# Loading small inputs as two rows each, and spreading them over the partitions with TensorE, in a one-token attention and mixer kernel

## The chip, the cores and the metric

The kernel runs on one core of a Trainium2 chip. The metric is device time in microseconds (us); lower is better.

## The reference, cut to what matters

```python
A: x (1,1,1024), k_cache and v_cache (1,4,65536,128), wq (1024,4096), wo (4096,1024)   # attention
B: B_x (1,1,1024), w_in (1024,3584), w_sp (1,1), b_sp (1,), w_out (1792,1024)          # gated MLP
gate_w (1024,)                                                                          # all bf16

x = A_x
g = sigmoid((x * gate_w).sum(-1))
a = softmax(x @ wq @ k.T / sqrt(128)) @ v @ wo         # 32 query heads, 4 KV heads
z = gelu(x @ w_in);  z1, z2 = halves of z
b = (z1 * (w_sp * layernorm(z2) + b_sp)) @ w_out
out = g * a + (1 - g) * b
```

There is one token. Nearly all the work is to read 162 MB of caches and weights once. The small inputs are x and gate_w (2 KB each) and the scalars w_sp and b_sp (2 bytes each).

## The kernel before

The big arrays go through a ring of five SBUF slots of up to 4 MB. SP issues their loads on its own DMA queue (q1), a load as soon as its slot has been used. ACT issues the four small loads at the start on another queue (q10). Every access is to one tensor called arena, so the profile tells inputs apart by the DRAM side or by line number.

```python
NS = 5                                    # slots in the ring
...
def small(dst, src, key): ...             # one DMA on ACT's queue
# x and gate_w: partition p gets elements 4p..4p+3 of each half: 256 pieces of 8 bytes
small(vw(xT, 0, [[4, 2], [1, 4]]), A_x[0, 0].rearrange("(i p k) -> p i k", i=2, k=4), "xT")
small(vw(gw, 0, [[4, 2], [1, 4]]), gate_w.rearrange("(i p k) -> p i k", i=2, k=4), "gw")
# the scalars: one element of DRAM read 128 times, once for each partition
small(wb[:, 0:1], bass.AP(tensor=B_w_sp.tensor, ..., ap=[[0, 128], [1, 1]]), "wsp")
small(wb[:, 1:2], bass.AP(tensor=B_b_sp.tensor, ..., ap=[[0, 128], [1, 1]]), "bsp")
...
# the first work, in program order (each engine works in this order)
DVE: z2 = xT * gw                         # L384, waits for x and gate_w
DVE: gs = sum over the free axis
PE:  sum over the partitions (matmul with ones)
ACT, DVE: g = 1 / (1 + exp(-gs)), 1 - g
DVE: xw = spread xT                       # L395
PE:  64 matmuls x @ wq                    # L404; they free the first two slots of the ring
...
DVE: transposes of the K tiles            # L449
PE:  scores                               # L457
```

Order of the loads: wq, wq, K, w_in, K, w_in, K, w_out, K, ..., then K and V in turn, then wo in six pieces.

## Time and profile before

| | before |
|---|---|
| time, median of 6 runs beside the changed kernel | 387.72 us (387.49 to 388.95) |
| span of the profiled execution | 385.9 us |
| small packets (q10) | 832 |
| x / gate_w / w_sp / b_sp landed, us after issue | 22.0 / 38.9 / 48.7 / 56.9 |
| wq matmuls start | 42.13 us |
| sixth load of the ring issued | 45.76 us |

From the page of the kernel before: its span; the DMA row (busy tenths in 40 slices of 9.65 us) and what the DMA engines moved in each slice; the queues, with packets, MB and share of 16 engines' time; and the chain of work that ended last, by engine.

```profile
span 385.9 us, 3595 instructions
...
DMA  8999999999999999999999999999999999999994
GB/s 326 435 435 442 374 442 426 429 436 433 435 408 419 435 435 430 428 435 427 431 431 435 433 435 431 435 423 429 435 431 426 428 432 435 430 431 428 419 419 190
...
q1 hardware_dynamic: 6200, 162.01, 98.1%
...
q10 hardware_dynamic: 832, 0.00, 0.1%
...
DMA 53%; PE 22%; DVE 22%; issue 1%; ACT 0%; ACTq 0%; DVEq 0%
```

The bulk queue occupies the DMA engines for 98.1% of the span. The stream is what the time consists of. Low slices are the fifth (38.6 to 48.2 us: 374) and the twelfth and thirteenth (106 to 125 us: 408 and 419).

The DMA issues of the four small loads: destination and source, issuing queue, size, and us from issue to landing.

```profile
arena<-in_A_x_dram ACTq DMA_DIRECT2D x1, 2.0 KB, 22.0
arena<-in_gate_w_dram ACTq DMA_DIRECT2D x1, 2.0 KB, 38.9
arena<-in_B_w_sp_dram ACTq DMA_DIRECT2D x1, 0.2 KB, 48.7
arena<-in_B_b_sp_dram ACTq DMA_DIRECT2D x1, 0.2 KB, 56.9
```

The chain of waits in order of time (start, duration, what), some of its pieces:

```profile
1.24 38.87 DMA arena<-in_gate_w_dram
...
42.13 6.39 PE pb L404 x64
...
51.27 1.26 DVE arena L449
...
371.10 11.62 DMA arena<-in_A_wo_dram
...
382.76 0.62 PE pb L635 x7
383.41 0.42 DVE arena L641
```

The chain begins with 39 us of waiting for 2 KB of gate_w, and ends with the last piece of wo. SP's own timeline shows how the ring bridges the first part: five loads at the start, the next only once the wq matmuls have freed a slot.

```profile
2.77 0.49 SPq L345 DMA_DIRECT2D arena<-in_A_k_cache_dram  x1
45.76 0.33 SPq L345 DMA_DIRECT2D arena<-in_B_w_in_dram  x1
48.54 0.33 SPq L345 DMA_DIRECT2D arena<-in_A_k_cache_dram  x1
```

### The profile page before, as it was taken

The page shows a single profiled execution, that of the slowest core. Times are in us where ns is not written, and L with a number is a line of the kernel's source. Part 1 is how long each engine was busy: PE and PEld are TensorE (multiplying, and loading weights), DVE is VectorE, ACT ScalarE, POOL GpSimd, SP SyncE. Part 2 cuts the span into 40 slices and gives each one's busy share as a digit, 9 for nine tenths or more (in the row PEclk, how much of TensorE's full clock was granted, in tenths as well). Part 3 has the DMA queues.
Part 4 walks back from the last instruction along what each step waited for, and adds up shares of the span by engine and source line. Part 5 has one row for each costly group of instructions (what it writes and reads, how often), then busy time and mean ns, then how long its engine had stood idle before and what let it go on. Part 6 is the DMA issues. An engine that isn't in the chain of part 4 may idle for free.

```text
span 385.9 us, 3595 instructions
## 1 busy us (share of the span) xinstructions
PE 227.0 (59%) x1542; PEld 84.7 (22%) x1542; DVE 210.5 (55%) x326; ACT 30.6 (8%) x71; POOL 2.1 (1%) x9
## 2 busy tenths in 40 slices
PE   0000668983886888472688383827883929543354
PEld 0000225562232222121222120212220202211121
DVE  4000078335999997574597574735984748511010
ACT  1000000001011110000010000000010100320000
POOL 2000000000000000000000000000000000000000
PEclk9999969695899999696789697956697978866555
DMA  8999999999999999999999999999999999999994
GB/s 326 435 435 442 374 442 426 429 436 433 435 408 419 435 435 430 428 435 427 431 431 435 433 435 431 435 423 429 435 431 426 428 432 435 430 431 428 419 419 190
DMA packets 7048, 162.24 MB, mean 420 GB/s; under 512 B 1524, under 2 KB 1528, under 8 KB 1784
## 3 DMA queue, kind: packets, MB, share of 16 engines
q1 hardware_dynamic: 6200, 162.01, 98.1%
q8 instruction: 12, 0.20, 0.2%
q10 hardware_dynamic: 832, 0.00, 0.1%
q14 instruction: 4, 0.03, 0.0%
HBM read 162.01 MB, written 0.00 MB: 420 GB/s over the span
## 4 chain that ended last, share of the span: by engine, by line
DMA 53%; PE 22%; DVE 22%; issue 1%; ACT 0%; ACTq 0%; DVEq 0%
DMA arena<-in_A_k_cache_dram 31%; DVE arena L449 16%; PE pb L457 13%; DMA arena<-in_gate_w_dram 10%; DMA arena<-in_A_v_cache_dram 9%; PE pb L543 3%; DMA arena<-in_A_wo_dram 3%; PE pb L501 2%; DVE arena L470 2%; PE pb L404 2%; DVE arena L492 1%; PE pb L635 1%; DVE arena L518 0%; DVE arena L438 0%; PE pb L523 0%
## 5 line engine op out<-in xcount | busy, mean ns | idle before, releaser
L457 PE MATMUL pb<-arena 128*128 128x512 bf16 x512 | 154.4, 442 | 78.5 <-DVE arena L449 76.2
L449 DVE STREAM_TRANSPOSE arena<-arena 128x1024 f32<-128x1024 f32 x128 | 151.3, 1216 | 56.7 <-DMA arena<-in_A_k_cache_dram 50.5
L457 PEld LDWEIGHTS pb<-arena 128*128 128x128 bf16 x512 | 45.4, 106 | 181.9 <-DVE arena L449 128.1
L501 PE MATMUL pb<-arena 128*32 128x512 bf16 x512 | 39.3, 442 | 20.3 <-DMA arena<-in_A_v_cache_dram 17.8
L487 ACT ACTIVATE arena<-arena 128x512 bf16<-128x512 f32 x32 | 23.0, 720 | 208.5 <-DVE arena L492 155.3
L492 DVE STREAM_TRANSPOSE arena<-arena 128x512 bf16<-128x512 bf16 x32 | 21.7, 679 | 18.3 <-PE pb L501 18.3
L470 DVE TENSOR_SCALAR_CACHE_REDUCE arena<-pb 128x512 f32<-128x512 f32 x32 | 21.7, 678 | 5.7 <-PE pb L457 5.5
L386 PE MATMUL pb<-arena 128*128 128x1 f32 x2 | 0.6, 364 | 40.6 <-DVE arena L385 40.6
L501 PEld LDWEIGHTS pb<-arena 128*32 128x32 bf16 x512 | 12.9, 107 | 44.5 <-issue 36.5
L384 DVE TENSOR_TENSOR arena<-arena 128x8 f32<-128x8 bf16 x1 | 0.2, 166 | 35.1 <-DMA arena<-in_gate_w_dram 35.1
L543 PEld LDWEIGHTS pb<-arena 128*128 128x128 bf16 x224 | 13.8, 161 | 0.4
L543 PE MATMUL pb<-arena 128*128 128x1 bf16 x224 | 13.7, 198 | 0.0
L635 PE MATMUL pb<-arena 128*1 128x256 bf16 x128 | 7.8, 409 | 6.3 <-DMA arena<-in_A_wo_dram 6.2
L515 DVE RECIPROCAL arena<-pb 128x1 f32<-128x1 f32 x4 | 0.7, 168 | 18.1 <-PE pb L513 18.1
L386 PEld LDWEIGHTS pb<-arena 128*128 128x128 f32 x2 | 0.5, 314 | 40.6 <-DVE arena L385 40.6
L641 DVE TENSOR_TENSOR arena<-pb,arena 97x256 bf16<-97x256 f32 x1 | 0.4, 425 | 13.4 <-PE pb L635 13.4
L404 PE MATMUL pb<-arena 128*2 128x512 bf16 x64 | 6.4, 584 | 0.9 <-DVE arena L395 0.9
L487 ACT ACTIVATION_READ_ACCUMULATOR arena<-arena 128x1 f32 x32 | 6.0, 186 | 0.0
L635 PEld LDWEIGHTS pb<-arena 128*1 128x1 bf16 x128 | 3.4, 109 | 10.5 <-DMA arena<-in_A_wo_dram 7.6
L523 PE MATMUL pb<-arena 128*128 128x128 bf16 x16 | 1.8, 243 | 5.2 <-DVE arena L518 5.2
L554 DVE COPY arena<-pb 128x28 f32<-128x28 f32 x1 | 0.2, 187 | 7.8 <-PE pb L543 7.8
L411 DVE CAST arena<-pb 98x512 bf16<-98x512 f32 x1 | 0.7, 692 | 6.5 <-PE pb L404 6.5
(81 smaller groups left out, 47.7 us busy)
## 6 DMA issues: line engine op xcount, KB each, us to landing
arena<-in_A_k_cache_dram SPq DMA_DIRECT2D x16, 4096.0 KB, 28.8
arena<-in_A_v_cache_dram SPq DMA_DIRECT2D x16, 4096.0 KB, 33.5
arena<-in_A_wq_dram SPq DMA_DIRECT2D x2, 4096.0 KB, 17.0
arena<-in_B_w_in_dram SPq DMA_DIRECT2D x2, 3584.0 KB, 27.4
arena<-in_A_wo_dram SPq DMA_DIRECT2D x3, 2048.0 KB, 34.6
arena<-in_B_w_out_dram SPq DMA_DIRECT2D x1, 3584.0 KB, 16.8
arena<-in_A_wo_dram SPq DMA_DIRECT2D x1, 1024.0 KB, 23.1
arena<-in_A_wo_dram SPq DMA_DIRECT2D x2, 512.0 KB, 13.1
```

Source lines behind the costliest of these rows:

```text
L386: P("PE", lambda e: e.matmul(pf(PTB)[:, 0:1], ones, col(C_GS), start=True, stop=True), r=["ones", "gs"], w=[B(PTB)])
L404: ins = e.matmul(pf(OB)[32 * cg:32 * cg + 2, :], xw[:, 3 * c + 1 - s:3 * c + 3 - s], sl[:, WQ_N * k + 512 * (4 * s + cg):WQ_N * k + 512 * ...
L411: P("DVE", lambda e: e.tensor_copy(qsb[0:98, :], pf(OB)[0:98, :]), w=[("psb", 0), B(OB)])
L449: P("DVE", lambda e: e.transpose(ktb(i).bitcast(F32), sl[:, 2048 * j:2048 * (j + 1)].bitcast(F32)), r=[key], w=[("kt", i % NKTS)])
L457: ins = e.matmul(pf(sb), qpad[g % 2][:, o:o + 128], vw(ktb(i), 64 * f2 + ev, [[128, 16], [2, 32]]), start=(j == 0 and fe == 0), stop=(j == ...
L470: P("DVE", lambda e: e.tensor_scalar(scs(n), pf(sb), 0.0, None, op0=ALU.add, op1=ALU.max, accum_out=maxc[:, n:n + 1]), w=[("sc", n % NSC), ...
L487: P("ACT", lambda e: e.activation(psb(n), scs(n), ACTF.Exp, bias=gcol(g, K_NB), scale=SCALE, accum_out=lp[:, n:n + 1]), r=[("sc", n % NSC) ...
L492: P("DVE", lambda e: e.transpose(ptsb(n), psb(n)), r=[("psb", n % 2)], w=[("ptsb", n % 2)])
L501: ins = e.matmul(pf(OB)[32 * cg:32 * (cg + 1), :], ptsb(n)[:, 32 * b:32 * (b + 1)], vw(sl, 128 * b, [[2048, 4], [1, 128]]), start=(u == 0 ...
L523: ins = e.matmul(pf(MB)[:, 0:128], sel[:, 128 * c:128 * (c + 1)], osc[:, 128 * c:128 * (c + 1)], start=(c == 0), stop=(c == 3))
L543: ins = e.matmul(pf(MB)[:, z:z + 1], vw(sl, c0, [[FC, 128]]), xT[:, 2 * i + k:2 * i + k + 1], start=(i == 0 and k == 0 and z == 0), stop=( ...
L635: ins = e.matmul(pf(FB)[32 * q:32 * q + 1, 0:QW], ovec[:, 8 * i + c:8 * i + c + 1], sl[:, o:o + QW], start=(i == 0 and c == 0), stop=(i == ...
```

## The change

x and gate_w are loaded as two rows of 512 elements, on two partitions. Four PE transposes bring x to the partitions; the gate product and sum are done on the two rows. The scalars are loaded once each, and a matmul with a row of ones spreads them. The aim is to have the small inputs early and with few packets. The order at the start of the program becomes: transposes of x, spread of the scalars, gate product, gate sum, wq.

```diff
-    small(vw(xT, 0, [[4, 2], [1, 4]]), A_x[0, 0].rearrange("(i p k) -> p i k", i=2, k=4), "xT")
-    small(vw(gw, 0, [[4, 2], [1, 4]]), gate_w.rearrange("(i p k) -> p i k", i=2, k=4), "gw")
-    small(wb[:, 0:1], bass.AP(tensor=B_w_sp.tensor, offset=B_w_sp.offset, ap=[[0, 128], [1, 1]]), "wsp")
-    small(wb[:, 1:2], bass.AP(tensor=B_b_sp.tensor, offset=B_b_sp.offset, ap=[[0, 128], [1, 1]]), "bsp")
+    small(xrow[0:2, :], A_x[0, 0].rearrange("(i n) -> i n", i=2), KX)
+    small(grow[0:2, :], gate_w.rearrange("(i n) -> i n", i=2), KG)
+    small(wb[0:1, 0:1], B_w_sp, "wsp")
+    small(wb[0:1, 1:2], B_b_sp.rearrange("(a n) -> a n", a=1), "bsp")
...
-    P("DVE", lambda e: e.tensor_tensor(z2[:, 0:KC], xT, gw, ALU.mult), ...)
-    P("DVE", lambda e: e.tensor_reduce(col(C_GS), z2[:, 0:KC], AXX, ALU.add), ...)
-    P("PE", lambda e: e.matmul(pf(PTB)[:, 0:1], ones, col(C_GS), start=True, stop=True), ...)
+    for c in range(4):                                                  # PE
+        ins = e.transpose(pbf(PTB)[:, 2 * c:2 * c + 2], vw(xrow, c, [[4, 128]], 0, 2), idb[0:2, 0:2])
+    P("DVE", ... tensor_copy(xT <- PTB)) ;  P("DVE", ... tensor_copy(xw <- xT))
+    P("PE", lambda e: e.matmul(pf(MB)[:, 0:2], oneb[0:1, :], wb[0:1, :], start=True, stop=True),
+      r=["oneb", "wsp", "bsp"], w=[B(MB)])
+    P("DVE", lambda e: e.tensor_copy(wbb, pf(MB)[:, 0:2]), ...)
+    P("DVE", lambda e: e.tensor_tensor(prod[0:2, :], xrow[0:2, :], grow[0:2, :], ALU.mult), ...)
+    P("DVE", lambda e: e.tensor_reduce(col(C_GS)[0:2, :], prod[0:2, :], AXX, ALU.add), ...)
+    P("PE", lambda e: e.matmul(pf(PTB)[:, 0:1], ones[0:2, :], col(C_GS)[0:2, :], start=True, stop=True), ...)
...
-    ... wb[:, 0:1] ... wb[:, 1:2]          # later, in the mixer
+    ... wbb[:, 0:1] ... wbb[:, 1:2]
```

More of the change, by code (lines that the diff above doesn't have):

```diff
@@ L189, in bass_gated_mix__gqa_block_cached__mixer_gmlp__decode_kernel @@
         ("QPAD", 2 * 4 * QP), ("IDB", 128), ("IDF", 256), ("BM", 256), ("ONES", 256), ("SEL", 16 * 32),
-        ("M16", 32), ("M8", 16), ("M32", 64), ("MQ", 32), ("OT", 256), ("XT", KC), ("GW", KC), ("WB", 2), ("MAXC", 2 * G * NU), ("LP", 2 * G * NU),
+        ("M16", 32), ("M8", 16), ("M32", 64), ("MQ", 32), ("OT", 256), ("XT", KC), ("WB", 2), ("WBB", 4), ("ONEB", 128), ("MAXC", 2 * G * NU), ("LP", 2 * G * NU),
         ("COLS", 2 * 64), ("DM", 32), ("QT", 32), ("QALL", 128), ("XW", 3 * KC), ("OSC", 512), ("OV", OC), ("Z", 2 * 28), ("Z2", 2 * 28),
@@ L211, in bass_gated_mix__gqa_block_cached__mixer_gmlp__decode_kernel @@
     m32, mq, ot = af("M32", 32), af("MQ", 16), af("OT", 128)
-    xT, gw, wb = ab("XT", KC), ab("GW", KC), ab("WB", 2)
+    xT, wb, wbb, oneb = ab("XT", KC), ab("WB", 2), af("WBB", 2), ab("ONEB", 128)
     qpad = [ab("QPAD", 4 * QP, 4 * QP * i) for i in range(2)]
@@ L256, in bass_gated_mix__gqa_block_cached__mixer_gmlp__decode_kernel @@
     P("DVE", lambda e: e.memset(ones, 1.0), w=["ones"])
+    P("DVE", lambda e: e.memset(oneb, 1.0), w=["oneb"])
     P("DVE", lambda e: e.memset(brow, 0.0), w=["brow"])
@@ L267, in f @@
                 return e.dma_start(dst, src)
-        P("ACT", f, w=[key], dma=key)
-    small(vw(xT, 0, [[4, 2], [1, 4]]), A_x[0, 0].rearrange("(i p k) -> p i k", i=2, k=4), "xT")
-    small(vw(gw, 0, [[4, 2], [1, 4]]), gate_w.rearrange("(i p k) -> p i k", i=2, k=4), "gw")
-    small(wb[:, 0:1], bass.AP(tensor=B_w_sp.tensor, offset=B_w_sp.offset, ap=[[0, 128], [1, 1]]), "wsp")
-    small(wb[:, 1:2], bass.AP(tensor=B_b_sp.tensor, offset=B_b_sp.offset, ap=[[0, 128], [1, 1]]), "bsp")
+        P("ACT", f, w=[key], dma="l%s" % (key if isinstance(key, str) else key[1]))
+    xrow, grow, prod = ab("SC", 512, (NSC - 2) * 1024), ab("SC", 512, (NSC - 3) * 1024), af("SC", 512, (NSC - 4) * 512)
+    KX, KG, KP = [("sc", NSC - i) for i in (2, 3, 4)]
+    small(xrow[0:2, :], A_x[0, 0].rearrange("(i n) -> i n", i=2), KX)
+    small(grow[0:2, :], gate_w.rearrange("(i n) -> i n", i=2), KG)
+    small(wb[0:1, 0:1], B_w_sp, "wsp")
+    small(wb[0:1, 1:2], B_b_sp.rearrange("(a n) -> a n", a=1), "bsp")
     stream = []
@@ L381, in bass_gated_mix__gqa_block_cached__mixer_gmlp__decode_kernel, with f @@
           r=["idb"], w=[KSE])
-    P("DVE", lambda e: e.tensor_tensor(z2[:, 0:KC], xT, gw, ALU.mult), r=["xT", "gw"], w=["z2"])
-    P("DVE", lambda e: e.tensor_reduce(col(C_GS), z2[:, 0:KC], AXX, ALU.add), r=["z2"], w=["gs"])
-    P("PE", lambda e: e.matmul(pf(PTB)[:, 0:1], ones, col(C_GS), start=True, stop=True),
+    def f(e):
+        for c in range(4):
+            ins = e.transpose(pbf(PTB)[:, 2 * c:2 * c + 2], vw(xrow, c, [[4, 128]], 0, 2), idb[0:2, 0:2])
+        return ins
+    P("PE", f, r=[KX, "idb"], w=[B(PTB)])
+    P("DVE", lambda e: e.tensor_copy(vw(xT, 0, [[4, 2], [1, 4]]), vw(pbf(PTB), 0, [[1, 2], [2, 4]])),
+      w=["xT", B(PTB)])
+    P("DVE", lambda e: e.tensor_copy(vw(xw, 1, [[3, KC]]), xT), r=["xT"], w=["xw"])
+    P("PE", lambda e: e.matmul(pf(MB)[:, 0:2], oneb[0:1, :], wb[0:1, :], start=True, stop=True),
+      r=["oneb", "wsp", "bsp"], w=[B(MB)])
+    P("DVE", lambda e: e.tensor_copy(wbb, pf(MB)[:, 0:2]), w=["wbb", B(MB)])
+    P("DVE", lambda e: e.tensor_tensor(prod[0:2, :], xrow[0:2, :], grow[0:2, :], ALU.mult), r=[KX, KG], w=[KP])
+    P("DVE", lambda e: e.tensor_reduce(col(C_GS)[0:2, :], prod[0:2, :], AXX, ALU.add), r=[KP], w=["gs"])
+    P("PE", lambda e: e.matmul(pf(PTB)[:, 0:1], ones[0:2, :], col(C_GS)[0:2, :], start=True, stop=True),
       r=["ones", "gs"], w=[B(PTB)])
@@ L392, in bass_gated_mix__gqa_block_cached__mixer_gmlp__decode_kernel @@
       r=["g"], w=["omg"])
-    P("DVE", lambda e: e.tensor_copy(vw(xw, 1, [[3, KC]]), xT), r=["xT"], w=["xw"])
     for i in range(4):
@@ L576, in mixer_piece @@
         P("DVE", lambda e: e.reciprocal(col(C_R1), col(C_S1)), r=["s1"], w=["r1"])
-        P("DVE", lambda e: e.scalar_tensor_tensor(col(C_AL), col(C_R1), 2.0, wb[:, 0:1], op0=ALU.mult, op1=ALU.mult),
-          r=["r1", "wsp"], w=["al"])
-        P("DVE", lambda e: e.tensor_copy(col(C_BE), wb[:, 1:2]), r=["bsp"], w=["be"])
+        P("DVE", lambda e: e.scalar_tensor_tensor(col(C_AL), col(C_R1), 2.0, wbb[:, 0:1], op0=ALU.mult, op1=ALU.mult),
+          r=["r1", "wbb"], w=["al"])
+        P("DVE", lambda e: e.tensor_copy(col(C_BE), wbb[:, 1:2]), r=["wbb"], w=["be"])
         P("DVE", lambda e: e.tensor_scalar(z2[:, 0:FC], ze[:, 0:FC], col(C_AL), col(C_BE), op0=ALU.mult, op1=ALU.add),
```

## The prediction

> **What bounds it now.** The DMA stream. The page's queue list has the bulk queue at 98.1% of 16 engines for 162.01 MB; the stretch view shows 431 GB/s from 118 to 360 us[...]. At 431 GB/s the bytes alone need 376 of the 385.9 us. PE is busy 59%, DVE 55%.
>
> **What the small loads cost.** x and gate_w go out as 256 pieces of 8 bytes each; with the two broadcast scalars the small queue has 832 packets. In the DMA issues x lands after 22.0 us, gate_w after 38.9, the scalars after 48.7 and 56.9. [...] x has 16 packets per engine, and 16 turns behind 32 KB bulk packets of about 1.22 us (packet records) make 19.5 of its 22.0 us. So in the chain of waits gate_w ends at 40.1 us, DVE idles 35.1 us before the gate product, and the wq matmuls start at 42.13, though the wq loads landed at about 12 and 21. K transposes start at 51.27; their load was there from about 31.
>
> **Why nearly all of it is hidden.** The ring holds five loads, about 46 us of stream. The sixth was issued at 45.76 us, just as the ring ran dry. Against 431 GB/s the stretches 40 to 45 (419), 45 to 50 (400), 50 to 104 (428), 104 to 108 (410) and 108 to 118 us (421; compute still catching up) are short by 0.14, 0.36, 0.38, 0.19 and 0.23 us: 1.3 us together. The chain gives gate_w 10% of the span, but removing that does not remove 39 us; the stream binds instead.
>
> **What changes.** Removed: about 830 small packets, a few tenths of a us of stream at most. Added: four small PE transposes, a tiny matmul, two PSUM copies, and a product and a sum over 2x512 in place of 128x8: 2 to 3 us in series (similar ones take 0.2 to 0.7), before the first wq load lands, so free. x and gate_w should land 3 to 5 us after issue (one or two turns of 1.22 us plus the 2.5 us that 22.0 leaves), the scalars within about 8.
>
> **What the profile after should show.** DVE's wait on small loads under 8 us (35.1). wq matmuls from 11 to 13 us. Sixth load issued at 15 to 18 us (45.76). First K transpose at 30 to 33 us. The dips at 45 to 50 and 104 to 118 us gone. From about 150 us on both traces agree but for a shift of about 1 us; the last wo load still ends the kernel, then about 3 us of PE, DVE and store.
>
> **Predicted time:** 387.75 - 1.3 = 386.4 us, range 385.6 to 387.4. Chances: faster by over 2% 0.01, within 2% 0.97, slower 0.02.
>
> **What would make it wrong.** Early work could be slower than the stream: K-only stages need about 10.5 us of DVE per pair against 9.7 us of stream, and PE at half clock needs more; if the ring fills there, dips move rather than vanish. The two-row loads may hold back the few DMA engines they use, or wait longer than one turn. If the deficit at 104 to 118 us is of the first V loads, not of the backlog, only about 0.9 us is gained.

From the prediction: 0.14 + 0.36 + 0.38 + 0.19 + 0.23 = 1.3 us, each from the stretch view. That the stream binds rests there on the 98.1% and the 376 us of bytes, and that small loads wait by turns on the packets of x. The half clock of its last paragraph is in the trace of before: from 85.2 to 98.9 us, for one, the granted clock was 0.5; a score matmul (L457) took 629 ns (median) at that clock and 378 at 1.0. Its few tenths of a us for the small packets are an estimate; the page has q10 at 0.1% of the 385.9 us, 0.4 us. Its 10.5 and 9.7 us are estimates too: eight transposes of 1.16 us and two reductions of 0.62 (from start to start at 59.50 to 64.77 us) make 10.5, and the 4.19 MB of a K load at 431 GB/s take 9.7.

## The result, and the profile after

| | before | after |
|---|---|---|
| median (range), 6 runs each | 387.72 us (387.49 to 388.95) | 386.63 us (386.58 to 386.90) |
| ratio, 95% interval | | 0.9969 (0.9956 to 0.9982) |
| small packets (q10) | 832 | 12 |
| wq matmuls start | 42.13 us | 15.25 us |
| sixth load issued | 45.76 us | 18.87 us |
| first K transpose | 51.27 us | 32.70 us |
| last piece of wo landed (chain of waits) | 382.72 us | 381.68 us |

A ratio is the mean time of one kernel's fast runs over that of the other's of the same rounds, so it is not quite the ratio of the medians quoted. The interval is a gain of 0.7 to 1.7 us, and the medians differ by 1.1 us.

The page of the changed kernel, the lines that answer to those of before:

```profile
span 384.9 us, 3607 instructions
...
GB/s 331 436 433 440 430 424 437 429 435 433 427 433 426 427 433 429 433 432 436 433 429 436 424 429 436 429 431 430 433 433 431 433 430 429 434 433 422 421 418 169
...
q1 hardware_dynamic: 6200, 162.01, 98.2%
...
q10 hardware_dynamic: 12, 0.00, 0.0%
...
DMA 71%; PE 16%; DVE 11%; issue 0%; SPq 0%
```

The fifth slice, 374 before, is 430; the twelfth and thirteenth, 408 and 419, are 433 and 426. The bulk queue's packets and bytes are the same.

The timeline of the start (start, duration, engine, line, operation, count, and the idle time before it with what ended it):

```profile
13.03 0.16 PE L396 MATMUL pb<-arena 1*128 1x2 bf16 x1 [10.14 <-DMA arena<-in_B_b_sp_dram]
13.23 0.16 DVE L398 COPY arena<-pb 128x2 f32<-128x2 f32 x1 [7.69 <-PE pb L396]
...
15.25 3.58 PE L419 MATMUL pb<-arena 128*2 128x512 bf16 x32
18.87 0.33 SPq L349 DMA_DIRECT2D arena<-in_B_w_in_dram  x1
23.00 3.21 PE L419 MATMUL pb<-arena 128*2 128x512 bf16 x32 [4.17 <-DMA arena<-in_A_wq_dram]
...
32.70 3.50 DVE L464 STREAM_TRANSPOSE arena<-arena 128x1024 f32<-128x1024 f32 x3 [3.71 <-DMA arena<-in_A_k_cache_dram]
```

All early work now waits for the bulk stream, except one thing: PE stands 10.14 us before the little matmul that spreads the scalars, for a b_sp that lands only at 13 us.

The end of the chain of waits:

```profile
370.06 11.62 DMA arena<-in_A_wo_dram
...
381.73 0.62 PE pb L650 x6
382.35 0.02 issue
382.37 0.42 DVE arena L656
```

It is the end of before, 1.04 us earlier. Nothing changed behind the last landing.

### Where in the stream the time was gained

The trace has records of the DMA packets; those of the bulk queue add up to the 162.01 MB that the page has as read. In the kernel before 4352 of its 6200 packets, with 88% of the bytes, are of 32 KB, and for 342 of the 385.9 us 16 bulk packets are under way at once, as one after another on each of 16 engines would give; a record does not name its engine. From these records, the time in us at which so many MB of the bulk queue had landed; 162.0 MB is the very end:

```
MB landed     before    after    gained
 10.0          26.91    26.54     0.38
 22.0          55.24    54.08     1.17
 44.0         106.63   105.56     1.07
 46.0         111.68   110.15     1.53
150.0         353.20   351.68     1.52
161.5         379.79   378.26     1.53
162.0         382.14   381.10     1.05
```

So the lead was gained before 112 us, and about a third of it did not survive to the last bytes. These are records of one execution each, and a single mark falls somewhere in a round of packets: b_swap (section 5), whose stream otherwise runs like that of before, is 0.3 us ahead at 46 MB and 0.05 at 47 MB. A difference of 0.2 to 0.3 us at one mark alone says nothing. Also from the records, the mean duration in ns of a bulk packet (scaled to 32 KB) by stretches of 4 us:

```
from us    4    8   12   16   20   24   28   32   36   40   44   48   52   56
before  1213 1228 1213 1213 1213 1213 1214 1217 1220 1247 1326 1231 1213 1213
after   1213 1213 1213 1213 1213 1213 1213 1213 1213 1221 1213 1216 1218 1239
```

Before has slow packets from about 42 to 49 us. It also has them at 104 to 112 us (1267 and 1259, where after has 1216), which is not in this table. The first place was the prediction's "ring running dry". But the records contradict that at once: in the kernel before, the fifth load was still landing until 51 us, and the sixth, issued at 45.76, was in time. Something else is slow there. What coincides with it is the w_sp load: its 128 small packets run from 40.3 us to about 50 us.

### The profile page after: what moved, and what is told of

It is laid out like the page before. It is cut to its first block, busy times and chain, and to the rows that moved or that the text cites. A ratio compares the mean times of both kernels' runs of the same rounds, so it can differ in the third digit from the quotient of the medians.

```text
span 384.9 us, 3607 instructions
## 1 busy us (share of the span) xinstructions
PE 233.6 (61%) x1547; PEld 86.2 (22%) x1547; DVE 211.6 (55%) x329; ACT 30.6 (8%) x71; POOL 2.1 (1%) x9
## 3 DMA queue, kind: packets, MB, share of 16 engines
q1 hardware_dynamic: 6200, 162.01, 98.2%
HBM read 162.01 MB, written 0.00 MB: 421 GB/s over the span
## 4 chain that ended last, share of the span: by engine, by line
DMA 71%; PE 16%; DVE 11%; issue 0%; SPq 0%
DMA arena<-in_A_k_cache_dram 59%; PE pb L472 11%; DMA arena<-in_A_v_cache_dram 10%; DVE arena L464 9%; DMA arena<-in_A_wo_dram 3%; PE pb L516 2%; PE pb L558 2%; DVE arena L485 1%; PE pb L650 1%; DVE arena L507 0%; DVE arena L533 0%; PE pb L538 0%; PE pb L528 0%; SPq L349 0%; PE pb L495 0%
## 5 line engine op out<-in xcount | busy, mean ns | idle before, releaser
L472 PE MATMUL pb<-arena 128*128 128x512 bf16 x512 | 160.0, 457 | 93.6 <-DVE arena L464 91.7
L472 PEld LDWEIGHTS pb<-arena 128*128 128x128 bf16 x512 | 46.7, 109 | 201.3 <-DVE arena L464 144.9
L558 PEld LDWEIGHTS pb<-arena 128*128 128x128 bf16 x224 | 13.8, 161 | 0.4
L656 DVE TENSOR_TENSOR arena<-pb,arena 97x256 bf16<-97x256 f32 x1 | 0.4, 425 | 13.4 <-PE pb L650 13.4
L650 PEld LDWEIGHTS pb<-arena 128*1 128x1 bf16 x128 | 3.4, 109 | 10.5 <-DMA arena<-in_A_wo_dram 7.6
```

The lines of the kernel that those rows point to most:

```text
L472: ins = e.matmul(pf(sb), qpad[g % 2][:, o:o + 128], vw(ktb(i), 64 * f2 + ev, [[128, 16], [2, 32]]), start=(j == 0 and fe == 0), stop=(j == ...
L558: ins = e.matmul(pf(MB)[:, z:z + 1], vw(sl, c0, [[FC, 128]]), xT[:, 2 * i + k:2 * i + k + 1], start=(i == 0 and k == 0 and z == 0), stop=( ...
L650: ins = e.matmul(pf(FB)[32 * q:32 * q + 1, 0:QW], ovec[:, 8 * i + c:8 * i + c + 1], sl[:, o:o + QW], start=(i == 0 and c == 0), stop=(i == ...
```

## The experiments

Two theories stood at first. "Cover" (the prediction's): the gain comes from work that starts earlier, so that the ring never runs short. "Packets": the gain comes from the small packets that are no longer sent, whatever the time at which work starts. The first four kernels ran on one chip beside the same nine runs of before (median 387.68 us).

### 1. Early start, all small packets kept (b_gate_late)

```diff
-    (gate product, sum, matmul, exp, ... before the wq matmuls)
+        if si == 1:          # after the scores of the second K tile
+            (the same gate product, sum, matmul, exp, ...)
```

> The kernel before, with all 832 small packets, but the gate chain (product, sum, matmul, exp) moved from before the wq matmuls to after the second K tile, so wq waits for x (about 22 us) and not for gate_w (about 40 us). Theory 'cover' (the gain comes from the bulk stream running short because work starts late): wq from about 22.5 us, sixth load at about 26 us, first K transpose at 31 to 33 us, no stretch under 425 GB/s between 40 and 120 us, time 386.8 to 387.1 us, so all of the gain but the 0.3 us of stream that the small packets take. Rival 'packets' (the gain comes from not sending the small packets, among them the shared w_sp element that is read 128 times from 40 to 51 us, just where the stream dips): the dip at 42 to 50 us stays at about 400 GB/s, time 387.4 to 387.7 us.

Measured: 387.85 us, ratio 1.0003 (0.9989 to 1.0017). No gain. SP's sixth load in the timeline of this run:

```profile
26.87 0.33 SPq L345 DMA_DIRECT2D arena<-in_B_w_in_dram  x1
```

The GB/s row of its page:

```profile
GB/s 326 435 435 430 387 435 430 428 436 435 433 431 435 435 419 431 428 435 427 428 431 431 433 428 435 435 433 436 428 431 426 428 432 424 433 435 435 414 420 168
```

The sixth load goes out 19 us earlier than before, and yet the fifth slice stays low (387). The bulk packets of 44 to 48 us took 1321 ns, before 1326. "Cover" falls as the explanation of that dip. The twelfth and thirteenth slices are full (431 and 435), and 0.5 us of lead is there from 46 MB on (111.18 us against 111.68), so the early start does something for that dip. But at the last byte the lead is gone: 382.16 against 382.14 us.

### 2. Late start, scalars loaded once (b_scal_new)

```diff
-    small(wb[:, 0:1], bass.AP(tensor=B_w_sp.tensor, ..., ap=[[0, 128], [1, 1]]), "wsp")
-    small(wb[:, 1:2], bass.AP(tensor=B_b_sp.tensor, ..., ap=[[0, 128], [1, 1]]), "bsp")
+    small(wb[0:1, 0:1], B_w_sp, "wsp")
+    small(wb[0:1, 1:2], B_b_sp.rearrange("(a n) -> a n", a=1), "bsp")
+    (spread by a matmul after q, read from wbb in the mixer, as in the change)
```

> The kernel before, with x and gate_w in 8-byte pieces as before, but the two scalars loaded once each and spread by a matmul (placed after q). Theory 'cover': wq still starts at about 42 us and the stream still dips at 42 to 50 and 104 to 118 us; time 387.4 to 387.7 us. Rival 'packets': the dip at 42 to 50 us is gone, since no w_sp reads fall there; time 386.9 to 387.2 us.

Measured: 387.08 us, ratio 0.9986 (0.9973 to 0.9998). SP's sixth load in the timeline:

```profile
45.94 0.33 SPq L347 DMA_DIRECT2D arena<-in_B_w_in_dram  x1
```

The GB/s row of the page:

```profile
GB/s 327 436 436 434 438 427 433 425 417 424 429 427 436 436 434 432 436 431 429 432 432 432 430 425 429 429 427 436 436 432 427 436 430 429 434 425 436 413 421 173
```

Work starts as late as before, and the fifth slice is full (438); the bulk packets of 44 to 48 us took 1216 ns. At 22 MB the stream is 0.76 us ahead of before. So the dip at 42 to 49 us belongs to the scalar loads. The dip at 104 to 118 us is gone too (427 and 436), and the lead grows there from 0.64 us at 44 MB to 1.08 at 46 MB, although work starts late. In the kernel before it was a near thing: the load issued at 105.14 us found, by an estimate from the sizes of the loads issued and the bytes landed, 1.2 MB still in flight, under 3 us of stream. Kernels with an early start (the change, b_gate_late and b_both) have 8.5 MB or more in flight at each of their loads between 96 and 116 us, and no such dip. But here the same load goes out at 104.03 us and finds, by the same estimate, 1.2 MB as well, so how near the ring is to dry does not tell the two late kernels apart. From 98 to 118 us before has 22 bulk packets over 1260 ns, b_swap, which starts as late, 13, this run 4, b_gate_late and the change one each. An early start removes this dip; why b_scal_new, started late, mostly escapes it is not shown.

The run also teaches a caution. Its stretch view for 42 to 50 us (busy times by engine, granted clock, DMA share, GB/s) reads:

```profile
42.00:50.00 8.00, 6.44 (x73) 2.30 (x73) 1.35 (x6) 0.00 (x0) 0.00 (x0) 1.00 0.93 401
```

401 GB/s looks like a dip, but no packet there was slow. 401 instead of 431 over 8 us is 0.24 MB, some seven packets of 32 KB, fewer than one round of the 16 engines. The engines work nearly in step (in the kernel before, between 42 and 49 us, 16 bulk packets start within 0.34 to 0.51 us, then none for 0.7 to 1.1 us), and where the edge of a short stretch falls among their packets decides the figure: in the changed kernel, a stretch of 8 us that begins at 41.4, 41.7, 42.0, 42.3, 42.6 or 42.9 us gives 426, 413, 433, 439, 422 or 423 GB/s. The packet durations are the safer reading.

### 3. x and gate_w as rows, scalars as before (a_scal_old)

```diff
     (the changed kernel)
-    small(wb[0:1, 0:1], B_w_sp, "wsp")
-    small(wb[0:1, 1:2], B_b_sp.rearrange("(a n) -> a n", a=1), "bsp")
-    (spread by a matmul)
+    (both broadcast by DMA to 128 partitions, as before)
```

> The changed kernel with x and gate_w as two rows, but the two scalars loaded 128 times each as before (no matmul for them). Theory 'cover': wq starts at about 12.5 us, no dips, time 386.6 to 386.8 us (288 small packets more than the changed kernel, about 0.1 us of stream). Rival 'packets': the stream dips to about 400 GB/s while the w_sp element is read 128 times, which now falls at about 8 to 20 us, and the time is 387.0 to 387.4 us.

Measured: 387.97 us, ratio 1.0008 (0.9995 to 1.0020). The whole gain of the change is gone, though this kernel keeps the early start and the two rows. The GB/s row:

```profile
GB/s 326 380 434 445 422 429 435 425 438 434 426 434 431 432 431 431 434 430 424 427 431 434 429 427 434 431 429 435 434 429 431 434 428 431 432 431 431 416 418 161
```

The low slice has moved to the second (9.7 to 19.3 us: 380), with the w_sp load. Bulk packets took 1349 ns at 8 to 12 us and 1313 at 12 to 16. At 6 MB this stream is 1.14 us behind before. The b_sp load that follows in the same form, at about 17 to 27 us, slows nothing (1213 ns).

### 4. Scalars' matmul moved behind q (a_scal_late)

```diff
     (the changed kernel)
-    (matmul that spreads the scalars, before the gate product)
+    (the same matmul, after q)
```

> The changed kernel with the scalars' matmul moved from before wq to after q, so PE no longer waits for the last small load (13.0 us). wq starts at 12.5 to 13 us (was 15.25), sixth load at 16 to 17 us (was 18.87). Theory 'cover': no change in time, 386.6 us within 0.15, since the ring holds work until about 46 us either way. Rival 'every us of late start counts': 2 us faster.

Measured: 386.58 us, ratio 0.9970 (0.9958 to 0.9983), like the changed kernel. wq starts at 13.05 us in place of 15.25, and SP's sixth load goes out here:

```profile
16.68 0.33 SPq L349 DMA_DIRECT2D arena<-in_B_w_in_dram  x1
```

So the wait for b_sp in the changed kernel costs nothing: 2.2 us at the start are not found in the time.

### 5. Which load is it? (b_swap, a_wsp8, a_bsp8, a_mix)

Why did the w_sp load slow the stream and the b_sp load not, in all runs so far? Either it is that tensor, or it is the place: w_sp came first.

```diff
 b_swap:  the kernel before
-    small(... B_w_sp ...) ; small(... B_b_sp ...)
+    small(... B_b_sp ...) ; small(... B_w_sp ...)
 a_wsp8, a_bsp8, a_mix:  the changed kernel, behind its four small loads
+    for jn, jt in enumerate([B_w_sp] * 8):        # a_bsp8: [B_b_sp] * 8; a_mix: twelve tensors
+        small(junk[:, 16 * jn:16 * jn + 1], bass.AP(tensor=jt.tensor, ..., ap=[[0, 128], [1, 1]]), ...)
```

> The kernel before with the two scalar broadcasts issued in the other order (b_sp first, then w_sp). The first four runs showed the stream's bulk packets slowed from 1213 to about 1320 ns just while w_sp was being read 128 times, and not in the 128 reads of b_sp after it. Theory 'tensor' (it is that read of that address): the slow packets move from 42-50 us to about 51-59 us. Rival 'position' (the first broadcast of 2-byte elements, or the K load that runs then): they stay at 42-50 us. Time 387.7 us either way.

> The changed kernel plus eight more broadcasts of w_sp (128 reads of the same 2 bytes each, into unused columns), behind the four small loads. Theory 'tensor': the stream is slowed for about 85 us, from about 13 us on, by about 1 us a broadcast (0.75 to 1.1 measured for one): 386.6 + 6 to 9 = 393 to 396 us. Rival 'packets as such' (any 1,150 small packets cost the same): the same as a_bsp8.

> The changed kernel plus eight more broadcasts of b_sp, the same in number, size and place as those of w_sp in a_wsp8. Theory 'tensor': bulk packets stay at 1213 to 1220 ns, time 386.6 to 387.0 us. Rival 'packets as such': the same as a_wsp8, several us slower.

> The changed kernel plus twelve broadcasts of one 2-byte element each, one after the other in the small queue (about 11 us each): w_sp, b_sp, gate_w, A_x, B_x, wq, k_cache, v_cache, w_in, w_out, wo, and w_sp again. Looked at by the duration of the bulk packets in each stretch. Theory 'tensor': slow packets (over 1300 ns) in the two stretches of w_sp and perhaps in some of the others, none in that of b_sp. Rival 'position': only in the first.

Measured (before: median 387.84 us of seven runs): b_swap 387.65 us, ratio 0.9995 (0.9978 to 1.0012). a_wsp8 388.56 us, ratio 1.0021 (1.0006 to 1.0036). a_bsp8 388.37 us, ratio 1.0015 (1.0000 to 1.0030). a_mix 388.89 us, once. Mean duration in ns of bulk packets, from the packet records:

```
from us    4    8   12   16   20   24   28   32   36   40   44   48   52
b_swap  1215 1220 1213 1214 1228 1213 1215 1219 1218 1261 1304 1219 1213
a_wsp8  1227 1300 1338 1239 1213 1213 1213 1213 1213 1223 1217 1222 1220
a_bsp8  1233 1356 1337 1213 1213 1213 1213 1213 1214 1225 1217 1221 1227
a_mix   1232 1373 1351 1213 1213 1213 1213 1213 1214 1217 1218 1222 1229
```

"Tensor" falls and "position" holds; the two kernels with eight broadcasts cost nearly the same, as the rival "packets as such" has it. With b_sp first, the slow packets stay at 42 to 49 us. Eight broadcasts of either scalar slow the stream once, during the first, and not in the seven that follow (up to 88 us). In a_mix, too, only the first of twelve is slow, though each reads another tensor. The expectation of 393 to 396 us for a_wsp8 was too high by over 4 us for this reason, and that of 386.6 to 387.0 us for a_bsp8 too low by over 1 us. Apart from the first, the extra small packets are cheap: in the packet records the gap between bulk packets is about 6 ns longer when a small packet stands in it (from start to start of 32 KB packets at 13.4 to 22 us, median: 1215 ns in before, with a piece of x in each gap, and 1209 in the changed kernel, with none).

### 6. What about the first load is slow? (a_distinct, a_same8)

```diff
     (the changed kernel, behind its four small loads)
+    a_distinct: small(junk[:, 0:1], gate_w[0:128].rearrange("(p k) -> p k", k=1), "junk0")   # 128 addresses
+    a_same8:    small(junk[:, 0:4], bass.AP(tensor=gate_w.tensor, ..., ap=[[0, 128], [1, 4]]), "junk0")  # 8 bytes
+    both, next: small(junk[:, 16:17], bass.AP(tensor=B_w_sp.tensor, ..., ap=[[0, 128], [1, 1]]), "junk1")
```

> What slows the first broadcast. The changed kernel plus two small loads: 128 different 2-byte elements of gate_w, one to a partition (about 6 to 17 us), then a broadcast of w_sp to 128 partitions (about 18 to 28 us). If reading one address 128 times is what slows the stream the first time, slow bulk packets (over 1300 ns) come at 18 to 28 us; if it is 2-byte pieces to all partitions, first time, they come at 8 to 15 us and not later.

> As a_distinct, but the first of the two loads is one 8-byte piece of gate_w read 128 times. If reading one address is what counts, slow bulk packets come at 8 to 15 us and not in the w_sp broadcast after it; if 2-byte pieces count, they come at 18 to 28 us, in the w_sp broadcast.

Measured, once each: 387.82 and 387.88 us. Bulk packets:

```
from us       4    8   12   16   20   24   28
a_distinct 1214 1310 1325 1223 1213 1213 1213
a_same8    1214 1319 1332 1230 1213 1213 1213
```

Both first loads are slow, and the w_sp load after them is not. So it is neither the repeated reading of one address (a_distinct reads 128 different ones) nor pieces of 2 bytes (a_same8 has 8). What is left, by elimination, is that it is the first load of one small piece for each of 128 partitions on this queue, beside a running stream. In the kernel before, 512 pieces of x and gate_w went ahead of it, two to a partition, and slowed the stream only slightly (1228 ns at 8 to 12 us; 1220 to 1272 in the other kernels that have these pieces). The first such load costs 0.7 to 1.3 us of stream (against before: 0.76 at 22 MB in b_scal_new, which has no such load, and 1.3 at 6 MB in a_mix, where it comes first). Why the first one costs, I could not settle.

### 7. A still later start (b_x_behind)

```diff
     (the kernel before)
+    small(vw(junk, 0, [[4, 2], [1, 4]]), gate_w.rearrange("(i p k) -> p i k", i=2, k=4), "junk0")
     small(vw(xT, 0, [[4, 2], [1, 4]]), A_x[0, 0]...)
```

> The kernel before with one more load of 256 eight-byte pieces (gate_w into unused columns) put in front of x, so 17 more turns of about 1.22 us before x can land. Tests what a still later start costs. The ring's five loads end at about 49 us; x lands at about 43, and gate_w has some 12 turns to go when the stream runs out, which then pass fast. Theory 'ring cover' (late work is free up to about 46 to 49 us, and costs us for us beyond): the bulk stream stands still for some 5 to 7 us from about 49 us on; time 392 to 395 us. Rival (start of work has slack well beyond the ring, or the loss is caught up later): under 389 us.

Measured: 397.65 us against 387.82, ratio 1.0252 (1.0236 to 1.0268). SP's sixth load in the timeline:

```profile
57.03 0.33 SPq L348 DMA_DIRECT2D arena<-in_B_w_in_dram  x1
```

The GB/s row of the page (slices of 9.9 us here):

```profile
GB/s 337 423 446 424 432 49 430 435 432 443 421 291 441 443 426 421 423 443 441 427 430 423 428 433 443 430 431 424 430 430 438 430 431 433 421 430 438 413 424 176
```

The stretch view from 50 to 60 us, with 78 GB/s as its last figure:

```profile
50.00:60.00 10.00, 6.75 (x66) 2.43 (x66) 1.27 (x7) 0.17 (x1) 0.00 (x0) 1.00 0.28 78
```

Here the ring does run dry. In the packet records the last bulk packets of the five loads end at 50.2 to 50.7 us and the next ones start at 57.98, and the stream is 7.8 us behind before at 22 MB. The backlog of work makes it run short a second time (291 in the twelfth slice), and it is 10.0 us behind at 46 MB. That is more than the 4 to 7 us expected, because the first gap was a little longer than estimated and the second had not been counted. So "cover" is right as a limit. The first packet came 0.95 us after the issue at 57.03, so by an estimate the sixth load has to go out by about 49 us, and a later one is dear; no run tried an issue between 46.2 and 57.03 us. The kernel before, at 45.76, stayed within that limit with some 3.5 us to spare, so the change had nothing to gain there.

The same run confirms the turns. While the stream runs, a piece of a small load takes about 1.2 us. Once it stands still, the rest of gate_w, all of w_sp and all of b_sp, 48 semaphore writes among them, pass between 50.2 and 50.9 us.

### 8. Early start and scalars loaded once, x and gate_w in pieces (b_both)

```diff
     (the kernel before)
     + the gate chain moved, as in b_gate_late
     + the scalars loaded once and spread by a matmul, as in b_scal_new
```

> The kernel before with x and gate_w still in 8-byte pieces, but the gate chain moved behind the second K tile (as in b_gate_late) and the scalars loaded once each and spread by a matmul (as in b_scal_new). Alone they gave +0.1 and -0.5 us. Theory 'two causes' (the first scalar broadcast costs about 0.75 us of stream, the near-dry stretch at 104 to 118 us 0.45 us, the turns of x and gate_w about 0.2 us): the stream is 1.2 us ahead at 150 us, time 386.7 to 387.1 us. Rival 'broadcast alone' (an early start never helps the end, which waits for the last DMA engine): 387.1 us, as b_scal_new.

Measured: 387.05 us against 387.82, ratio 0.9979 (0.9966 to 0.9991). The interval overlaps that of b_scal_new (0.9986), so the time does not decide between the two. Nor does the stream show a gain by the early start: b_both is 1.29 us ahead of before at 150 MB and b_scal_new 1.12, a difference no larger than the scatter of one mark, and at the last byte both have 0.7 us (0.72 and 0.74). The early start adds little if anything on the way and nothing at the end.

### The parts put together

Gained against before in us, at 22 MB, at 150 MB and at the last byte of the bulk queue (packet records of one execution each), with the ratios of the timed runs:

| kernel | start | scalars | x, gate_w | 22 MB | 150 MB | last byte | ratio |
|---|---|---|---|---|---|---|---|
| b_gate_late | early | 128 each | pieces | -0.08 | 0.53 | -0.02 | 1.0003 |
| a_scal_old | early | 128 each | rows | -0.19 | 0.15 | -0.38 | 1.0008 |
| b_scal_new | late | once | pieces | 0.76 | 1.12 | 0.74 | 0.9986 |
| b_both | early | once | pieces | 0.75 | 1.29 | 0.72 | 0.9979 |
| the change | early | once | rows | 1.17 | 1.52 | 1.05 | 0.9969 |
| a_scal_late | early | once | rows | 1.13 | 1.57 | 0.97 | 0.9970 |

Kernels with the scalars loaded once are ahead; those with 128 packets each are not. The rows of x and gate_w seem to add 0.2 to 0.4 us of stream, but only where the scalars are loaded once: compare the change and a_scal_late with b_both, and a_scal_old, which has the rows and gains nothing, with b_gate_late. These are one execution each, and the intervals of the ratios overlap, so this part is not shown as firmly as that of the scalars. All early kernels lose about 0.5 us of lead between 161.5 MB and the last byte, and b_scal_new loses 0.3. There the time is that of the slowest of 16 DMA engines, not of the mean: in the last load the engines' semaphore writes lie 1.99 us apart in before and 2.58 us in the changed kernel. Which events make one engine late in one kernel and another in the next was not settled.

## Why the prediction was right or wrong

The time was right: 386.4 us predicted, 386.63 measured, inside the range. A good part of the reason was wrong.

- **"The stream binds", and removing gate_w from the chain "does not remove 39 us": right.** The start moved by 27 us (42.13 to 15.25) and the time by 1.1. a_scal_late and b_gate_late show the same: 2.2 us, and 19 us, of earlier start without any gain.
- **Small loads wait by turns: right in kind, mis-sized for the new kernel.** In the kernel before, the 256 pieces of x go out in 15 rounds of 16 (one of 32) from 3.63 to 21.16 us, about 1.22 us from round to round, the time of a bulk packet. In the trace after, the small packets from gate_w's first on come at 6.09, 7.35, 8.87, 10.08, 11.30 and 12.51 us (the second row's, at 6.40 and 7.65, aside), 1.21 to 1.26 us apart and once 1.52, and every second one has 4 bytes. These are semaphore writes: the trace has as many updates of the loads' semaphores, each 0.31 to 0.38 us after such a packet. Two rows gave two data packets and two semaphore writes, one element one and one, 12 packets for the four loads. I had counted a turn for the data and none for the semaphore. gate_w missed its 3 to 5 us as well: issued at 1.31 us, it sent its first packet only at 6.09 and its last semaphore write at 7.65, and why it waited for more than one turn was not looked into. So the steps "x and gate_w should land 3 to 5 us after issue" (for gate_w) and "the scalars within about 8" failed: b_sp, issued at 1.88, was usable at 13.03 us, wq started at 15.25 (predicted 11 to 13), the sixth load went out at 18.87 (15 to 18). x beat its 3 to 5 us, since its packets (2.17 and 2.20 us, 44 ns each) waited for no bulk packet; one starts 2 ns after the end of each (2.22 and 2.25): the transposes ran at 2.60 us. None of this cost time.
- **"The sixth was issued at 45.76 us, just as the ring ran dry": the step that failed.** The fifth load was landing until 51 us, and the first packets of the sixth started at 50.0, so the ring had not run dry. The slow stretch at 42 to 49 us was the first scalar broadcast beside the stream. b_gate_late keeps the dip with an early start, b_scal_new loses it with a late one, a_scal_old moves it to 8 to 16 us.
- **The sum of 1.3 us from five stretches: the right size in part by chance.** Short stretches of the GB/s view are uncertain by a good part of a round of 16 packets (section 2: 401 in place of 431 GB/s was seven). The terms for 40 to 50 us (0.14 and 0.36) were costed to the late start and belong to the broadcast, which is worth 0.76 us at 22 MB in b_scal_new, its turns included. The term for 50 to 104 us (0.38) answers to nothing: the lead is 1.17 us at 22 MB (55 us) and 1.07 at 44 MB (106 us). The terms for 104 to 118 us (0.19 and 0.23) were a real lead of about 0.46 us at 46 MB. b_gate_late gets it by the early start, but b_scal_new gets as much (0.44) with a late one, for a reason that is not shown, and b_gate_late has none of it left at the last byte. So neither these terms nor those for 40 to 50 us were gained by the path that the sum gives them, and that they add up to nearly the measured gain is luck.
- **Small packets "a few tenths of a us of stream at most": right** for turns as such (about 6 ns each), wrong as a statement about the loads, since the first broadcast alone cost two to three times as much.
- **The added work is free: right.** It lies before 16 us, and moving part of it (a_scal_late) changed nothing.
- **"From about 150 us on both traces agree but for a shift of about 1 us": right.** The last chain is the same, 1.04 us earlier.

## What to carry to other kernels

When a stream of large loads binds the kernel, a long wait at the head of the chain of waits is worth only what the stream loses by it (here the start moved by 27 us and the time by 1.1); ask until when the loads already in flight last, and take that from the packet records, not from the time of the next issue. Look at what small transfers do to the stream while they run, not only at when they land: here 128 pieces for one scalar cost more time than all of the late start, and loading the scalar once with a matmul to spread it gave most of the gain. A prediction can hit the time and miss the cause, so take each part of a change alone before you reuse its reason.
